# Third pair's q and k halves copied into the operands four steps later, in a one-core attention and mixture-of-experts kernel

## The chip, the cores and the metric

The kernel runs on one core of a Trainium2 chip. The metric is the time of one execution in microseconds (us) on the device. TensorE is called PE here, VectorE DVE, ScalarE ACT, GpSimd POOL and SyncE SP. SP computes nothing: it starts DMA transfers, one after the other, in the order in which the program lists them.

## What is computed

Four sequences of 768 tokens go through attention with eight heads of 64 columns. A query sees only the keys that fall to the same of 16 centroids. The result is the input of a mixture of eight experts, of which each token takes two.

```python
q_assign = np.argmax(np.einsum('bhsd,hcd->bhsc', q_n, c_n), axis=-1)
k_assign = np.argmax(np.einsum('bhsd,hcd->bhsc', k_n, c_n), axis=-1)
mask = q_assign[:, :, :, None] == k_assign[:, :, None, :]
scores = scale * np.matmul(q, k.transpose(0, 1, 3, 2))
scores = np.where(mask, scores, -1000000000.0)
scores = scores - np.max(scores, axis=-1, keepdims=True)
attn = np.exp(scores)
attn = attn / (np.sum(attn, axis=-1, keepdims=True) + 1e-09)
return np.matmul(attn, v).astype(np.float32)
# ... x = heads side by side; then, for each expert e of a token's top two:
h = np.maximum(x[mask] @ w1[e], 0.0)
out[mask] += top2_w[mask, k, None] * (h @ w2[e])
```

## The kernel before

**Pairs and steps.** Attention goes by pairs of heads, 16 in all, numbered p = 0 to 15. A pair takes 12 steps: for each of its two heads (s = 0, 1) six blocks of 128 keys. Step t computes scores and their exponentials for one block (`scores`, L506: two matmuls, one on operand A and one on operand B, for each half of the 768 queries, then an ACT exponential, L515), and adds the block of four steps earlier to the output (`values`, L529). Pair 0 owns steps 0 to 11, pair 1 steps 12 to 23, pair 2 steps 24 to 35. Everything a pair needs beforehand is laid beside the steps of the pairs ahead of it.

**What a pair needs.** `load_qk` (L316) brings q and k of four heads from HBM with two DMAs. `a_split` (L374) transposes one head's q or k on PE (L381) and splits it into a high half (ACT, L390) and a low half (DVE, L391), both written to the tile `hl`; four calls fill `hl` for a pair. `b_place` (L457) then copies `hl` within SBUF into the operands A and B of the pair, with ten DMAs on SP (all at L455, the helper `dma`). `b_mask` (L469) copies the centroid marks `mk` into A with four DMAs. `b_max` (L475) multiplies parts of A and takes row maxima on DVE (L483, L486), and `b_negT` (L497) turns the negated maxima (L500, ACT L502 into `nt`) and copies them into two rows of B with one DMA. `scores` of a head can't run on B before those two rows are in.

**Buffers.** There are three A and three B, so pair p uses number p % 3. In the order listings below, A_151, A_152 and A_153 are those of pairs 0, 1 and 2, and B_154, B_155 and B_156 likewise. `hl` exists once (pair 1 alone uses a tile called `xt`), so `a_split` of pair 3 overwrites the `hl` from which `b_place` of pair 2 copies. `qk` has two buffers. All PSUM results but the outputs go through a ring of six banks.

**What sets the order.** The table `AT` (L24) gives each call a step, relative to w = 12 * (p - 2). `attention` (L182) files the calls under their steps in thirds of a step and emits them in that order, and each engine and SP runs its own in that order. For the calls around the change the steps come out as: pair 2's `b_place` at 0.333 - 0.667 = -0.333; pair 0's second `b_negT` (maxima of its second head, first used by `scores` in step 6) at -24 + 27.333 = 3.333; `load_qk` of the second sequence's first four heads at 24 - 20.667 = 3.333; pair 2's `b_mask` at 6.333; pair 3's first `a_split` at 12 - 4.667 = 7.333; pair 2's first `b_max` at 9.333.

Of the kernel before, what the change touches and what calls it, by code (L numbers as in the profile page):

```python
# [31 lines left out]
    bmax=9.333, neg=20.333, negT=22.0, zero=27.0, zstep=12.0, zlist=15.667, store=2.667, log=1.667, log2=3.0,  # L32
    logstep=0.667, turn=7.667, list=23.0, lstep=[2.0, 2.0, 1.0], bstep=1.0,
    gate=7.667, gstep=0.333, am=5.333, amstep=0.333, ky=4.0, cut=[13, 20], gplace=17.333,
    vd=[1, 1, 2, 3, 4, 5], sec=-6.0, qf=-4.0, place1=4.333,
    fv=[{'v': -5.0, 'vscale': 13.0, 'am': 24.333, 'amstep': 0.333, 'vsplit': 25.333, 'vstep': 2.0},
        {'v': 9.0, 'vscale': 11.667, 'am': 13.333, 'amstep': 0.333, 'vsplit': 15.0, 'vstep': 1.0}],
    thr=0.333, bmax1=14.667, bstep1=0.5)
# [6 lines left out]
class Kernel:  # L45
# [136 lines left out]
    def attention(self, ctx):  # L182
# [18 lines left out]
        def at(step, f, *a):  # L201
            sched.setdefault(divmod(round(3 * step), 3), []).append((f, a))

        def chain(step, by, fs):
            for i, f in enumerate(fs):
                at(step + by * i, f)


        T = AT
        for p in range(NP):  # L210
            b, hp = divmod(p, H // 2)
            w = 12 * (p - 2)
            if hp == 0:
                for g in range(2):
                    at(w + T["qk"] + 24 * g + (T["qf"] if (b, g) == (0, 1) else 0), self.load_qk, b, g)
                    v = w + 24 * g
                    V = T["fv"][g] if p == 0 else T
                    at(v + V["v"], self.load_v, b, g)
                    for h in range(0, 4, 2):
                        at(v + V["vscale"] + V["amstep"] * h, self.v_max, b, g, h)  # L220
                    chain(v + V["am"], V["amstep"], self.v_scale(b, g))
                    for h in range(4):
                        at(v + V["vsplit"] + V["vstep"] * h, self.v_split, b, g, h)
            P = T["first"] if p == 0 else T
            w += (0, T["sec"], T["thr"])[p] if p < 3 else 0
            for i in range(4):
                at(w + P["split"][i], self.a_split, p, i // 2, i % 2)
            if p == 0:
                at(w + P["sims"][0], self.c_turn)
            at(w + P["place"] + (T["place1"] if p == 1 else 0), self.b_place, p)  # L230
            for s in range(2):
                at(w + P["sims"][s], self.a_sims, p, s)
            for s in range(2):
                at(w + P["sum"][s], self.a_sum, p, s)
            for k, f in (("max1", self.a_max1), ("ge", self.a_ge), ("ky", self.a_ky), ("max2", self.a_max2),
                         ("eq", self.a_eq), ("mask", self.a_mask), ("bmask", self.b_mask)):
                at(w + P[k], f, p)
            if p == 0:
                for s in range(2):
                    for j in range(NJ):  # L240
                        at(w + P["bmax"][s] + P["bstep"][s] * j, self.b_max, p, s, j)
                    at(w + P["neg"][s], self.b_neg, p, s, 1)
                    at(w + P["negT"][s], self.b_negT, p, s, 1)
            else:
                w = 12 * (p - 2)
                bm, bs = (T["bmax1"], T["bstep1"]) if p == 1 else (T["bmax"], T["bstep"])
                for s in range(2):
                    for j in range(NJ):
                        at(w + bm + bs * (6 * s + j), self.b_max, p, s, j)
                at(w + T["neg"], self.b_neg, p, 0, 2)  # L250
                at(w + T["negT"], self.b_negT, p, 0, 2)
            if hp == H // 2 - 1:
                z = w + 36 + L
                if b + 1 == B:
                    continue
                at(z + T["store"], self.store_x, b)
                for jj in range(NJ):
                    at(z + T["log"] + T["logstep"] * jj, self.g_logits, b, jj)
                    at(z + T["log2"] + T["logstep"] * jj, self.g_logits2, b, jj)
                at(z + T["turn"], self.g_turn, b)  # L260
                fs = self.g_gate(b)
                chain(z + T["gate"], T["gstep"], fs[:self.GP])
                chain(z + T["gplace"], T["gstep"], fs[self.GP:])
                for j in range(2 * NJ):
                    at(z + T["list"] + T["lstep"][b] * j, self.g_list, b, j)
# [26 lines left out]
        for t in range(min(sched)[0], z + L + 2):  # L292
# [8 lines left out]
            if 0 <= u < z:  # L301
                p, s, kc = u // 12, (u % 12) // 6, u % 6
# [902 lines left out]
```

## Time and profile before

| | |
|---|---|
| median of 3 runs | 1111.88 us (1110.49 to 1113.07) |
| the profiled execution | 1111.9 us, of which 1110.1 us are the span of its instructions |
| PE busy | 1044.8 us, 94% of the span |
| DVE, POOL, ACT busy | 660.2, 542.2 and 484.3 us |
| mean granted TensorE clock | 0.981 |

The span runs from the first to the last instruction of the core. The remaining 1.8 us lie around it. Busy shares are means over the whole span, while the change lies in its first tenth, so the argument reads stretches of a few microseconds there: the order of SP's DMAs, the rows of single instructions with the idle time ahead of them, and the DMA traffic and clock by the microsecond.

### The profile page before, as it was taken

The page shows a single profiled execution, that of the slowest core. Times are in us where ns is not written, and L with a number is a line of the kernel's source. Part 1 is how long each engine was busy: PE and PEld are TensorE (multiplying, and loading weights), DVE is VectorE, ACT ScalarE, POOL GpSimd, SP SyncE. Part 2 cuts the span into 40 slices and gives each one's busy share as a digit, 9 for nine tenths or more (in the row PEclk, how much of TensorE's full clock was granted, in tenths as well). Part 3 has the DMA queues.
Part 4 walks back from the last instruction along what each step waited for, and adds up shares of the span by engine and source line. Part 5 has one row for each costly group of instructions (what it writes and reads, how often), then busy time and mean ns, then how long its engine had stood idle before and what let it go on. Part 6 is the DMA issues. An engine that isn't in the chain of part 4 may idle for free.

```text
span 1110.1 us, 22397 instructions
## 1 busy us (share of the span) xinstructions
PE 1044.8 (94%) x8709; PEld 815.9 (74%) x8709; DVE 660.2 (59%) x1412; ACT 484.3 (44%) x962; POOL 542.2 (49%) x598
## 2 busy tenths in 40 slices
PE   5789999999999999889999999999999999999994
PEld 4678898889889988765775766856757668567573
DVE  5777686977697868876365435444454354444411
ACT  2457767676767676562133323232233232322300
POOL 8257675789678968712324232341242323412311
PEclk8899999999999999899999999999999999999998
DMA  7776767666757655052235324441353243422200
GB/s 205 167 176 150 174 157 198 147 175 156 202 141 183 154 143 151 13 174 100 70 120 188 105 89 144 129 152 63 124 170 100 85 148 125 153 67 87 58 32 33
DMA packets 87056, 144.46 MB, mean 130 GB/s; under 512 B 13689, under 2 KB 65273, under 8 KB 86434
## 3 DMA queue, kind: packets, MB, share of 16 engines
q1 hardware_dynamic: 73650, 106.61, 36.0%
q0 software_dynamic: 13296, 36.38, 9.9%
q8 instruction: 70, 1.15, 0.4%
q14 instruction: 40, 0.33, 0.1%
HBM read 78.21 MB, written 26.51 MB: 94 GB/s over the span
## 4 chain that ended last, share of the span: by engine, by line
PE 72%; DVE 11%; issue 8%; POOL 2%; ACT 2%; DMA 2%; SPq 1%; POOLq 0%; DVEq 0%; ACTq 0%
PE ring L1105 20%; PE ring L1144 19%; PE ring L514 9%; PE ring L483 5%; PE av L543 3%; PE av L549 2%; PE av L545 2%; PE ring L1095 2%; DVE aux L486 2%; PE ring L402 2%; PE ring L381 2%; DMA A<-mk 1%; DVE mm L486 1%; PE ring L417 1%; POOL out L1157 1%
## 5 line engine op out<-in xcount | busy, mean ns | idle before, releaser
L526 POOL TENSOR_TENSOR pl<-pe 128x768 f16<-128x768 f32 x173 | 251.8, 1470 | 82.7 <-ACT pe L515 80.5
L1105 PE MATMUL ring<-xT,w1t 128*128 128x416 f16 (+2 forms) x1536 | 274.4, 340 | 0.2 <-DVE xT L1010 0.2
L1144 PE MATMUL ring<-w2t,hT 128*128 128x512 f32 x1152 | 273.0, 393 | 0.0
L1144 PEld LDWEIGHTS ring<-w2t,hT 128*128 128x128 f32 x1152 | 213.3, 188 | 43.5
L1105 PEld LDWEIGHTS <-w1t 128*128 128x128 f16 x1536 | 149.9, 98 | 121.8 <-issue 5.4
L515 ACT ACTIVATE pe<-ring,l 128x384 f32<-128x384 f32 x384 | 201.5, 578 | 65.3 <-PE ring L514 55.7
L1157 POOL DMA_INDIRECT out<-yo,idx x52 | 62.8, 1208 | 233.6 <-DVE yo L1153 144.3
L486 DVE TENSOR_REDUCE aux<-ring 128x1 f32<-128x384 f32 x192 | 108.0, 562 | 74.5 <-PE ring L483 67.1
L514 PE MATMUL ring<-A 128*128 128x384 f32 x384 | 142.0, 370 | 0.7 <-ACT pe L515 0.7
L514 PE MATMUL ring<-B 128*128 128x384 f32 x384 | 130.6, 340 | 2.7 <-DMA B<-nt 2.7
L1153 DVE SCALAR_TENSOR_TENSOR yo<-ring,we,xt 128x512 f32<-128x512 f32 (+1 forms) x49 | 36.8, 750 | 156.5 <-PE ring L1144 133.7
L1114 ACT ACTIVATE hT<-ring 128x416 fp32r<-128x416 f32 (+3 forms) x128 | 56.7, 488 | 166.3 <-PE ring L1105 147.2
L483 PE MATMUL ring<-A 128*128 128x384 f32 x384 | 109.1, 360 | 12.1 <-DMA A<-mk 3.9
L1115 DVE SCALAR_TENSOR_TENSOR hT<-ring,hT 128x416 fp32r<-128x416 f32 (+3 forms) x128 | 66.1, 553 | 80.3 <-ACT hT L1114 74.4
L1084 POOL DMA_INDIRECT xg<-xs,idx x52 | 54.2, 1041 | 116.8 <-PE ring L1095 100.3
L486 DVE TENSOR_REDUCE mm<-ring 128x1 f32<-128x384 f32 x192 | 105.2, 548 | 0.0
L1009 ACT ACTIVATE xT<-ring,sx 128x512 f16<-128x512 f32 (+1 forms) x56 | 35.7, 653 | 150.5 <-PE ring L1095 150.5
L543 PE MATMUL av<-vv,pe 128*128 128x65 f16 x1152 | 98.0, 195 | 2.9 <-DVE xt L557 2.9
L545 PE MATMUL av<-vv,pe 128*128 128x64 f16 x1152 | 97.0, 193 | 0.0
L543 PEld LDWEIGHTS <-pe 128*128 128x128 bf16 x1152 | 80.4, 99 | 18.1 <-issue 11.8
L483 PEld LDWEIGHTS ring<-A 128*128 128x128 f32 x384 | 70.8, 193 | 24.0 <-ACT pe L515 10.1
L545 PEld LDWEIGHTS <-pe 128*128 128x128 bf16 x1152 | 78.6, 99 | 0.3
(205 smaller groups left out, 1423.8 us busy)
## 6 DMA issues: line engine op xcount, KB each, us to landing
stg<-in_moe_w SPq DMA_DIRECT2D x64, 512.0 KB
A<-hl SPq DMA_DIRECT2D x30, 384.0 KB
B<-hl SPq DMA_DIRECT2D x30, 384.0 KB
vt<-in_v SPq DMA_DIRECT2D x8, 768.0 KB
out<-zt SPq DMA_DIRECT2D x12, 512.0 KB
xs<-xt SPq DMA_DIRECT2D x4, 1536.0 KB
A<-hl SPq DMA_DIRECT2D x60, 96.0 KB
B<-hl SPq DMA_DIRECT2D x30, 192.0 KB
```

The source lines that it names most:

```text
L483: nc.tensor.matmul(t, A[:, 0, s, j * 128:j * 128 + 128], A[:, 1, s, n * 384:n * 384 + 384], start=True, stop=True)
L486: nc.vector.tensor_reduce(o, t, axis=X, op=OP.max, negate=True)
L514: nc.tensor.matmul(t, M[:, 1 - qi, s, ks], M[:, qi, s, ns], start=not qi, stop=bool(qi))
L515: nc.scalar.activation(pe[:, n], t, AF.Exp, bias=self.l64[:, 0:1], scale=self.scale)
L526: (nc.vector if last else nc.gpsimd).tensor_tensor(lo, pe, hi, op=OP.subtract)
L543: nc.tensor.matmul(av[:, j, :], ph[:, js], vv[:, hh, kj, 64:129], start=(kc == 0 and j == 0), stop=False, skip_group_check=True)
L545: nc.tensor.matmul(av[:, j, :64], ph[:, js], vv[:, hh, kj, 0:64], start=False, stop=False, skip_group_check=True)
L1105: nc.tensor.matmul(p, self.w1t[:, wi, c, f * 128:f * 128 + 128], self.xT[:, xi, c, n0:n1], start=(i == 0), stop=(i == 3 * ND - 1))
L1114: nc.scalar.activation(h0, x, AF.Relu)
L1115: nc.vector.scalar_tensor_tensor(h1, x, 0.0, h0, op0=OP.max, op1=OP.subtract)
L1144: nc.tensor.matmul(p, self.hT[:, hi, f, t * 128:t * 128 + 128], self.w2t[:, wi, f], start=(i == 0), stop=(i == 3 * NF - 1))
L1157: i = nc.gpsimd.indirect_dma_start(out=self.out, out_offset=bass.IndirectOffsetOnAxis(ap=en[:r], axis=0), in_=yo[:r], in_offset=None, boun ...
```

## The change

One number of the table goes, and a tuple takes its place. Pair 1's offset of 4.333 stays as it was; pair 0's is zero; pair 2's `b_place` moves by 4.0 steps, from -0.333 to 3.667.

```diff
-    vd=[1, 1, 2, 3, 4, 5], sec=-6.0, qf=-4.0, place1=4.333,
+    vd=[1, 1, 2, 3, 4, 5], sec=-6.0, qf=-4.0, later=(0, 4.333, 4.0),
...
-            at(w + P["place"] + (T["place1"] if p == 1 else 0), self.b_place, p)
+            at(w + P["place"] + (T["later"][p] if p < 3 else 0), self.b_place, p)
```

The lists of PE, DVE, ACT and POOL keep every instruction in its place. Only SP's list changes. Before, on SP, behind the marks of pair 1 (A_152<-mk), stood the ten copies of pair 2 (eight rows, of which the last two are shown) and then the second maxima of pair 0, the loads and the marks of pair 2:

```order
L455 DMA B_156<-hl 64x4x384
L455 DMA B_156<-hl 32x4x384
L455 DMA B_154<-nt 2x6x128
L323 DMA qk<-in_q 128x4x384
L323 DMA qk<-in_k 128x4x384
L455 DMA A_153<-mk 16x2x384 x4
```

Now, on SP, between the marks of pair 1 and the copies of pair 2 (the first four of their eight rows are shown):

```order
L455 DMA A_152<-mk 16x2x384 x4
L455 DMA B_154<-nt 2x6x128
L323 DMA qk<-in_q 128x4x384
L323 DMA qk<-in_k 128x4x384
L455 DMA A_153<-hl 64x4x384
L455 DMA A_153<-hl 32x2x384 x2
L455 DMA B_156<-hl 64x4x384
L455 DMA B_156<-hl 32x4x384
```

Three DMAs, the maxima and the two loads of 768 KB each, have moved ahead of the ten copies; the marks of pair 2 and all that follows stand behind the copies as before.

On ACT the list is the same before and now. This is the place where pair 3's first `a_split` stands, with what each instruction waits for (DMAHW are the counters of SP's DMAs, which go round eight of them):

```order
L449 ACTIVATE mk<-ring,ms 128x768 [waits DMAHW3_49,DMAHW2_49,DMAHW4_49,DMAHW1_49,PE_49]
L515 ACTIVATE pe<-ring,l_123 128x384 [waits PE_49,Pool_49]
L515 ACTIVATE pe<-ring,l_123 128x384 [waits PE_49]
L369 ACTIVATE vt<-vt,am 128x384
L370 ACTIVATE vv<-vt 128x6x64 [waits Activation_49]
L390 ACTIVATE hl<-ring 128x384 [waits DMAHW4_49,DMAHW3_49,DMAHW5_49,DMAHW2_49,DMAHW6_49,DMAHW1_49,DMAHW7_49,DMAHW0_49,PE_49]
L390 ACTIVATE hl<-ring 128x384 [waits PE_49]
```

Nothing moved here: the first L390 of pair 3 waits for all eight counters, which are those of the ten copies that read `hl`, and the copies are what has moved on SP.

## Rows read from the trace of the kernel before

**Rows 1.** Cores' view, and the page's line of PE busy times.

```profile
core 0: 1110.1 us, clock 0.981
PE 1044.8 (94%) x8709; PEld 815.9 (74%) x8709; DVE 660.2 (59%) x1412; ACT 484.3 (44%) x962; POOL 542.2 (49%) x598
```

**Rows 2.** Chain that ended last, 55 to 100 us: start, us, what.

```profile
58.28 3.67 DMA B<-nt
...
62.00 1.33 PE ring L514 x3
...
68.42 0.48 ACT hl L390
68.93 0.57 DVE hl L391
...
69.54 0.71 PE ring L483 x2
```

**Rows 3.** SP's timeline: start, us, engine, line, operation, out<-in, count.

```profile
23.48 0.58 SPq L323 DMA_DIRECT2D qk<-in_q  x1
24.10 0.56 SPq L323 DMA_DIRECT2D qk<-in_k  x1
...
47.64 2.91 SPq L455 DMA_DIRECT2D A<-hl  x3
...
56.89 1.29 SPq L455 DMA_DIRECT2D B<-hl  x2
58.28 1.30 SPq L455 DMA_DIRECT2D B<-nt  x1
...
65.72 3.06 SPq L455 DMA_DIRECT2D A<-mk  x4
69.52 0.37 SPq L331 DMA_DIRECT2D vt<-in_v  x1
74.27 0.67 SPq L455 DMA_DIRECT2D B<-nt  x1
...
76.76 2.86 SPq L455 DMA_DIRECT2D A<-hl  x3
```

**Rows 4.** ACT's timeline, at pair 0's second maxima.

```profile
52.82 0.25 ACT L502 ACTIVATE nt<-ring 12x128 fp32r<-12x128 f32 x1
```

**Rows 5.** PE's timeline; in brackets the idle time before and its releaser.

```profile
35.98 0.82 PE L447 MATMUL ring<-identb,oh 128*128 128x128 bf16 x6 [3.04 <-DVE oh L438]
...
49.09 0.66 PE L483 MATMUL ring<-A 128*128 128x384 f32 x2 [1.75 <-POOL pl L526]
...
62.00 0.69 PE L514 MATMUL ring<-B 128*128 128x384 f32 x1 [2.74 <-DMA B<-nt]
...
69.01 0.33 PE L514 MATMUL ring<-B 128*128 128x384 f32 x1
...
72.72 0.51 PE L483 MATMUL ring<-A 128*128 128x384 f32 x2
```

**Rows 6.** By microsecond: us, PE, PEld, DVE, ACT, POOL busy, PEclk, DMA share, GB/s.

```profile
41.00:42.00 1.00, 1.00 (x6) 1.00 (x6) 1.00 (x3) 0.23 (x1) 0.00 (x0) 0.80 0.96 241
...
60.00:61.00 1.00, 0.00 (x0) 0.00 (x0) 0.00 (x0) 0.00 (x0) 0.49 (x1) 1.00 0.88 186
...
62.00:63.00 1.00, 1.00 (x3) 1.00 (x4) 0.00 (x0) 0.22 (x1) 0.00 (x0) 0.50 0.90 333
63.00:64.00 1.00, 1.00 (x7) 0.69 (x6) 0.32 (x1) 0.94 (x2) 0.00 (x0) 0.50 1.12 402
64.00:65.00 1.00, 1.00 (x17) 1.00 (x16) 0.70 (x2) 0.33 (x1) 0.92 (x1) 0.50 1.03 384
65.00:66.00 1.00, 1.00 (x16) 1.00 (x14) 0.18 (x1) 0.66 (x1) 0.55 (x1) 0.85 1.02 359
66.00:67.00 1.00, 1.00 (x8) 0.96 (x7) 0.97 (x3) 0.59 (x2) 0.00 (x0) 1.00 0.11 30
...
90.00:91.00 1.00, 1.00 (x31) 1.00 (x28) 1.00 (x3) 0.62 (x2) 1.00 (x1) 1.00 0.27 62
```

## The prediction, made before the changed kernel ran

> **What bounds the kernel now.** I read the busy times first: PE is busy for 94% of the span at a mean clock of 0.981 [rows 1], so for most of the run a delay of PE at one place is a delay of the end. The change moves only SP's DMAs around 48 to 70 us, so I then followed the chain that ended last through that stretch. It goes through SP: the ten copies of pair 2 hold SP from 47.64 to 58.18 us, the DMA of pair 0's second maxima is started behind them at 58.28 and lands 3.67 us later, and PE goes on at 62.00 [rows 2, 3]. ACT had those maxima ready at 52.82 + 0.25 = 53.07 us [rows 4]. PE's row at 62.00 names the price: 2.74 us idle, waiting for B<-nt [rows 5]. There is a second price in the clock column: the granted clock is 0.50 of full, which is the 1.2 GHz level, in the three microseconds after that idle time, 0.85 in the fourth and 1.00 from 66 us [rows 6]. That is 3.3 us at half speed behind the restart, with PE busy throughout, so some 1.65 us of work were lost. So the wait costs 2.74 + 1.65 = 4.4 us in all.
>
> Then I looked for who waits for the ten copies. The order listing says it: pair 3's first split, L390 on ACT, waits for all of them, since it overwrites the `hl` they read. In the trace before it starts at 68.42, and the first low half (L391 on DVE) follows; PE's next matmul behind them starts at 69.54 [rows 2]. The copies were long done by then: the maxima queued right behind them had landed at 58.28 + 3.67 = 61.95. So this wait costs nothing now, with 6.5 us to spare.
>
> **What the change removes.** The maxima no longer stand behind the copies. SP is free from the marks of pair 1 on, so their DMA starts at about 53.1 us. PE wants them at 62.00 - 2.74 = 59.26, 6 us later; even the 3.67 us of the queued case fits. The idle time goes and so does the drop of the clock: 4.4 us by the time PE and ACT come to pair 3's first split. ACT would be there at 68.42 - 4.4 = 64.0 us.
>
> **What it adds.** The copies now start later and behind more. SP starts the maxima at 53.1 (0.7 us, as the row at 74.27), then the two loads of q and k (0.58 and 0.56 us as at 23.48 and 24.10), then the first copy at about 55.2 us [rows 3]. How long do ten copies take? Before, 47.64 to 61.95 = 14.3 us [rows 2, 3]. Pair 3's went from 76.76 to about 90.3, by the microsecond in which the traffic ends, that is 13.5 us [rows 3, 6]. They are bound by the traffic, not by SP: at 186 GB/s the DMA engines were already 0.88 busy [rows 6]. If nothing else were in the way they would end at 55.2 + 14.3 = 69.5 us. But the two loads are now ahead of them. Before, these ran behind the copies, in 62.0 to 66.1, 4.1 us at a DMA share of 0.9 to 1.1 [rows 6], so they leave no room beside them. They are started 1.3 us ahead of the first copy, so they push the copies back by 4.1 - 1.3 = 2.8 us: the end is at 72.3 us.
>
> The lowest end I see is 55.2 + 13.5 = 68.7 (the shorter row and no delay by the loads), the highest 55.2 + 14.3 + 4.1 = 73.6 (no head start). I take 72.3, because the maxima of before, the one DMA that stood behind other traffic in this stretch, landed only when that traffic was over.
>
> **The new wait.** ACT comes to L390 at 64.0 and can start it at 72.3. Its queue is in order, so the exponentials of the following steps stand behind it; DVE waits in L391 likewise, with maxima queued behind; PE's ring of six banks fills with what these two don't take away. PE can finish step 8's scores (the last at 69.01 + 0.33 before, so about 65.0 now [rows 5]) and then stands still until L390 and L391 are through, 69.54 - 68.42 = 1.1 us after L390 starts. That is some 8.4 us of idle PE, in place of the 2.74 that went.
>
> Compared at the same instruction, L390 is at 72.3 instead of 68.42: **+3.9 us**, bounds 68.7 - 68.42 = +0.3 and 73.6 - 68.42 = +5.2. This comparison already contains the 4.4 us gained, since the end of the copies, not ACT's arrival, decides.
>
> **The clock.** After 2.74 and 3.04 us of idle PE the clock was at 0.50, after 1.75 us it was not [rows 5, 6]. So 8.4 us will halve it again, now behind the restart. In the row at 41 us (0.80) the half-speed stretch that began before PE's restart at 35.98 ends at about 41.4, so there it lasted 5.4 us, 2.7 us of work. I take **+1.65 us**, the loss of the case at 62 us, since it is the same work and nearest; bounds 0 and +2.7.
>
> **Other queues moved past.** Pair 2's marks still stand behind the copies on SP. Before they started at 65.72 [rows 3], waiting for ACT. Now they follow the copies and their data (196 KB of small rows) comes behind them, at about 72.3 + 1 = 73.4 us. The first matmul that reads them (pair 2's first maxima, at 72.72 before [rows 5]) comes 3.2 us behind the one at 69.54, that is at 72.72 + 3.9 + 1.65 = 78.3 now: covered by 5 us. If that cover were gone it would cost what it is late, microsecond for microsecond. The v load (69.52 before) starts at about the same time as before and is needed later. The loads of q and k arrive earlier, which nobody waits for. POOL stands still with the others and its work is no more than before.
>
> **Sum.** Profiled execution 1111.9 us (span 1110.1), next to the median of 1111.88: +3.9 + 1.65 = +5.5, so **1117.4 us**. By the bounds of the two terms +0.3 to +7.9, 1112.2 to 1119.8. What follows is driven by the same chain (SP's next DMA of maxima waits for ACT, the copies of pair 3 wait for that), and PE is nearly full from there, so I expect nothing to give the delay back.
>
> **Rivals.**
> *Faster: the copies are quick.* If ten copies within SBUF moved as fast as the loads do (333 to 402 GB/s in 62 to 66 us [rows 6], twice the 186 of the copies), 13.4 us of traffic would be 6.5, and with the loads not in the way they would be done at 55.2 + 1 + 6.5 = 62.7, ahead of ACT's 64.0. Then the whole 4.4 us is kept: 1107.5 us. It decides in favour of this if the copies end within 8.8 us of their first start. Against it stand both rows, 13.5 and 14.3, and a DMA share of 0.88 at 186 GB/s.
> The Trainium skill, page "DMA: Bandwidth & Descriptors", section "Where 436 GB/s comes from", says that transfers from SBUF to SBUF are bound by the fabric at 435 GB/s; by that an estimate of 3.9 MB for the loads and copies would be over in some 9 us, which gives about 1108 us. The trace doesn't agree: in the copies it moved 186 GB/s at a DMA share of 0.88.
>
> *Same: a break-even.* The copies run beside the loads and end at 68.7 to 69.5, and the clock's drop costs no more than a microsecond. Then L390 is 0.3 to 1.1 us later than before and the result is 1112.2 to 1114. For it: the bound of 68.7 exists. Against it: DMA shares add up to over 1, and PE would still stand for over 4 us, more than the 2.74 that halved the clock.
>
> *Slower than forecast: the marks are last.* If the marks landed after 78.3 us, pair 2's maxima would wait too. They are started at about 70 us behind the tail of the copies; landing 3 us beyond the point would give 1120.4. The 3.67 us that the maxima took behind the copies [rows 2] speaks against it.
>
> **How the numbers follow.** Forecast 0.75; faster rival 0.06; same 0.12; marks last or a long half-speed stretch 0.07. The difference that a measurement of this kernel can tell is about 0.2%, 2.2 us: faster means under 1109.7, slower over 1114.1. From the cases: faster 0.06, same 0.12, slower 0.82. The range leaves out the faster rival, half of the same case and most of the slowest: 1113.0 to 1120.0.
>
> **What would show it.** Right: PE's idle time ahead of B<-nt near 59 us is gone and the clock stays at 1.00 there; SP's ten copies start near 55 and pair 3's L390 near 72 us after a long idle time of ACT, with PE, DVE and POOL idle too; then a clock of 0.50 for some microseconds. Wrong: L390 before 68 us (the copies were quicker, or the loads don't delay them); or the delay at L390 is there and the end isn't late, which would mean slack further on that I haven't seen.

## The result and the profile after

The changed kernel takes 1120.34 us (median of 6 runs, 1118.49 to 1122.21) against 1112.05 us of the kernel before in the same set: a ratio of 1.0079, 95% interval 1.0063 to 1.0095. It is slower, as forecast, by 8.3 us where 5.5 were forecast, and just outside the range that ended at 1120.0. A second set gave 1119.77 us, ratio 1.0064 (1.0048 to 1.0081). The profiled execution took 1120.32 us.

The cores' view of after, beside the first line of [rows 1]:

```profile
core 0: 1118.5 us, clock 0.975
```

SP's timeline of after (start, us, engine, line, operation, out<-in, count), beside [rows 3]:

```profile
52.81 0.67 SPq L455 DMA_DIRECT2D B<-nt  x1
53.58 0.38 SPq L323 DMA_DIRECT2D qk<-in_q  x1
54.02 0.49 SPq L323 DMA_DIRECT2D qk<-in_k  x1
54.56 2.08 SPq L455 DMA_DIRECT2D A<-hl  x3
...
64.27 1.69 SPq L455 DMA_DIRECT2D B<-hl  x2
66.07 3.85 SPq L455 DMA_DIRECT2D A<-mk  x4
70.01 0.53 SPq L331 DMA_DIRECT2D vt<-in_v  x1
81.51 0.68 SPq L455 DMA_DIRECT2D B<-nt  x1
```

The maxima of pair 0 start 5.5 us earlier than before and the copies 6.9 us later. PE's timeline of after, beside [rows 5], and the chain that ended last, beside [rows 2]:

```profile
58.81 0.33 PE L514 MATMUL ring<-B 128*128 128x384 f32 x1
...
75.01 1.01 PE L483 MATMUL ring<-A 128*128 128x384 f32 x2 [9.57 <-DVE hl L391]
...
79.96 0.51 PE L483 MATMUL ring<-A 128*128 128x384 f32 x2
```

```profile
65.35 8.38 DMA B<-hl
73.88 0.50 ACT hl L390
74.40 0.57 DVE hl L391
75.01 1.01 PE ring L483 x2
```

The row at 58.81 is the matmul on B that waited 2.74 us before: it has no idle time ahead of it now. The row at 75.01 is the one that stood at 69.54 before. It has 9.57 us of idle time, and the chain goes through the last of the ten copies, which lands at 65.35 + 8.38 = 73.73 us, and through pair 3's first split right behind it. ACT's own row of that split, the first high half of pair 3, shows the wait from ACT's side:

```profile
73.88 0.87 ACT L390 ACTIVATE hl<-ring 128x384 fp32r<-128x384 f32 x2 [9.50 <-DMA A<-mk]
```

ACT came to it at 73.88 - 9.50 = 64.38 us. This row names the marks of pair 2 (A<-mk) as the releaser, the chain names the copies. The marks follow the copies on SP and use the same eight counters, and the profile infers its releasers; in the first experiment L390 starts before all of the marks are started, so it doesn't need them. By the microsecond (columns as in [rows 6]):

```profile
53.00:54.00 1.00, 1.00 (x6) 0.71 (x5) 0.90 (x3) 0.87 (x2) 1.00 (x2) 1.00 0.00 0
54.00:55.00 1.00, 0.85 (x4) 0.35 (x3) 1.00 (x3) 0.29 (x2) 1.00 (x2) 1.00 0.55 48
55.00:56.00 1.00, 0.48 (x3) 0.47 (x3) 1.00 (x3) 0.47 (x1) 1.00 (x2) 1.00 0.73 218
56.00:57.00 1.00, 0.51 (x3) 0.19 (x1) 1.00 (x3) 0.82 (x2) 0.46 (x1) 1.00 1.07 404
...
58.00:59.00 1.00, 1.00 (x18) 1.00 (x15) 0.89 (x3) 0.00 (x0) 1.00 (x2) 1.00 0.88 278
...
67.00:68.00 1.00, 0.00 (x0) 0.00 (x0) 0.00 (x0) 0.00 (x0) 0.00 (x0) 1.00 1.08 231
...
70.00:71.00 1.00, 0.00 (x0) 0.00 (x0) 0.00 (x0) 0.00 (x0) 0.00 (x0) 0.50 1.14 191
...
76.00:77.00 1.00, 1.00 (x14) 0.94 (x13) 1.00 (x3) 0.30 (x1) 1.00 (x1) 0.50 0.00 0
78.00:79.00 1.00, 1.00 (x5) 1.00 (x4) 0.47 (x2) 0.49 (x1) 0.00 (x0) 0.50 0.00 0
79.00:80.00 1.00, 1.00 (x7) 1.00 (x7) 0.46 (x1) 0.54 (x2) 0.00 (x0) 0.96 0.00 0
```

All five engines' columns are at zero around 67 to 71 us while the DMA engines are full; the granted clock halves during the wait (0.50, the 1.2 GHz level) and stays there until about 79 us, 4 us behind PE's restart.

### The profile page after: what moved, and what is told of

Read it like the earlier page. It is cut to its first block, busy times and chain, and to the rows that moved or that the text cites. A ratio compares the mean times of both kernels' runs of the same rounds, so it can differ in the third digit from the quotient of the medians.

```text
span 1118.5 us, 22393 instructions
## 1 busy us (share of the span) xinstructions
PE 1048.3 (94%) x8709; PEld 817.7 (73%) x8709; DVE 660.6 (59%) x1412; ACT 484.8 (43%) x962; POOL 542.7 (49%) x598
## 4 chain that ended last, share of the span: by engine, by line
PE 73%; DVE 11%; issue 8%; DMA 2%; POOL 2%; ACT 2%; SPq 1%; POOLq 0%; DVEq 0%; ACTq 0%
PE ring L1105 20%; PE ring L1144 19%; PE ring L514 9%; PE ring L483 5%; PE av L543 3%; PE av L549 2%; PE av L545 2%; PE ring L381 2%; PE ring L402 2%; PE ring L1095 2%; DVE aux L486 2%; PE ring L417 1%; DVE mm L486 1%; SPq L455 1%; POOL out L1157 1%
```

## The experiments

The theory: pair 3's first split waits for the end of pair 2's copies, and the two loads that now stand ahead of the copies push that end out. The rivals: copies that are started late are slow by themselves; something behind them in the queue delays their landing; the clock, not the wait, makes the loss. All experiments are read by one number, the time from SP's first copy of pair 2 to the start of the split's first L390 on ACT (19.3 us in the changed kernel, 54.56 to 73.88), because that number does not depend on when an execution reaches this place.

**Loads behind the copies.** The copies move by 3.667 instead of 4.0 steps, which puts them ahead of the loads.

```diff
-    later=(0, 4.333, 4.0),
+    later=(0, 4.333, 3.667),
```

> Pair 2's copies stand behind pair 0's second maxima as in the change, but ahead of the two loads of q and k instead of behind them. Theory (pair 3's first split waits for the end of the copies, and the loads ahead of them pushed that end out): the copies start at 53.6 us and end 14.3 us later, so the split's L390 starts near 67.9 instead of 73.88 us; PE still idles about 4 us, the clock still halves, and the time is about 1 us over the kernel before, near 1113 us. Rival A (the loads don't matter, copies started this late are slow by themselves, 19 us as in the changed kernel): L390 near 72.8 and about 1119 us. Rival B (the dependence of the split on the copies is not what costs): the time stays at 1120 us.

Rows of this kernel's SP and ACT timelines:

```profile
55.12 2.95 SPq L455 DMA_DIRECT2D A<-hl  x3
...
68.41 2.51 SPq L455 DMA_DIRECT2D A<-mk  x4
```

```profile
69.53 0.87 ACT L390 ACTIVATE hl<-ring 128x384 fp32r<-128x384 f32 x2 [3.56 <-DMA B<-hl]
```

That is 14.4 us, against 19.3: the loads ahead of the copies cost the difference. L390 starts at 69.53 while SP is still starting the marks (68.41 to 70.92), so it is not the marks that it waits for. The time was another matter: 1117.15 us, ratio 1.0049 (1.0035 to 1.0063), not 1113. The marks of pair 2 now stand behind the loads; pair 1's maxima were started at 78.56 us, 1.9 us later than in the timed profile of the next kernel, and the halved clock lasted from 70 to 77 us. The timed runs also scatter from 1114 to 1119 us, and of that the one profile (1114.98 us) shows only the lower end, so why the median is 4 us over the forecast is not fully explained.

**Loads far behind.** The loads go to the other side of pair 1's maxima, so that only marks and the v load follow the copies.

```diff
-  at(w + T["qk"] + ..., self.load_qk, b, g)
+  at(10.333 if (b, g) == (1, 0) else w + T["qk"] + ..., self.load_qk, b, g)
```

> As the change, but the two loads of q and k go far behind, to the other side of pair 1's maxima, so that nothing but marks and the v load follows the copies. Theory: copies from 53.6 us, L390 near 67.9 us, as with the loads right behind. Rival (transfers queued behind the copies also push their end out): L390 earlier here than with the loads right behind, by up to 2 us. If the tail is pushed out by the marks and the v load alone, L390 is near 69.5 in both.

> The kernel with the two loads behind pair 1's maxima again, now timed, as the reference of the next. L390 14.5 us behind the first copy, about 1113.8 us.

Rows of the second, timed kernel's profile:

```profile
55.02 2.97 SPq L455 DMA_DIRECT2D A<-hl  x3
```

```profile
69.44 0.87 ACT L390 ACTIVATE hl<-ring 128x384 fp32r<-128x384 f32 x2 [3.48 <-DMA A<-mk]
```

First copy to L390 took 55.38 to 69.92 = 14.5 us in one profile and 55.02 to 69.44 = 14.4 us in the other, timed at 1112.88 us, ratio 1.0013 (1.0001 to 1.0024). So loads that follow the copies don't delay them (the marks and the v load follow them in both kernels), and moving the copies alone, without the loads ahead, costs about 1 us: the wait at the split (PE idle 3.52 us) is then a little longer than the 2.74 us that the change removed.

**The v load later.** To see whether the v load behind the marks delays the last copy, it goes behind pair 1's maxima.

```diff
-  {'v': 9.0, 'vscale': 11.667, ...
+  {'v': 10.333, 'vscale': 11.667, ...
```

> As the change, with one more move: the v load that followed pair 2's marks goes behind pair 1's maxima, so that it is not in the queue while the copies end. In the changed kernel the last copy landed at 73.73 us although the traffic up to 72 us already covers loads, copies and marks. If the v load delayed that landing, L390 starts near 72.2 us here; if not, at 73.9 us as before. The v load itself now comes late for the maxima of v, which can cost some 2 us further on and says nothing on the question.

56.15 to 74.76 = 18.6 us. The unchanged order gave 19.3 and, in its second profile below, 18.5. The v load is not the cause. The total of 1123.99 us, a single run, contains the later maxima of v (PE idle 2.2 us for them).

**Loads earlier.** The loads go ahead of pair 0's maxima, where SP was idle, so they are through before the copies start.

```diff
+  at(2.667 if (b, g) == (1, 0) else w + T["qk"] + ..., self.load_qk, b, g)
```

> As the change, but the two loads of q and k go ahead of pair 0's second maxima on SP, so they are started some 5 us earlier and are through before the copies start. Theory (the loads cost only while they are in the queue ahead of the copies): first copy to pair 3's L390 takes 14.4 us, as with the loads behind (14.4 and 14.5 us measured), against 19.3 in the change; the marks of pair 2 have no loads ahead of them either, so about 1113.5 us. Rival (what costs is that the copies come late on SP, whatever is ahead of them): 19 us from the first copy to L390 and 1120 us.

```profile
54.01 2.96 SPq L455 DMA_DIRECT2D A<-hl  x3
```

```profile
69.38 0.87 ACT L390 ACTIVATE hl<-ring 128x384 fp32r<-128x384 f32 x2 [3.35 <-DMA A<-mk]
```

That is 15.4 us, and the time is 1114.59 us, ratio 1.0033 (1.0015 to 1.0051). Late copies are not slow by themselves: that rival falls. The loads were started 6.2 us ahead of the first copy here, and their traffic ended as it was started: nearly all of their cost is gone. The 0.9 us over 14.5 are not explained.

**Half the load.** Only the load of q stays ahead of the copies. The load of k, left out of `load_qk` here, becomes a call of its own, `load_k` (not shown), behind pair 1's maxima.

```diff
+                    if (b, g) == (1, 0):
+                        at(10.333, self.load_k, b, g)
...
+                if i and (b, g) == (1, 0):
+                    continue
```

> As the change, but only the load of q stays ahead of the copies; the load of k goes behind pair 1's maxima. Theory (the copies end later by the whole traffic of what was queued ahead, with no allowance for the head start): first copy to L390 takes 14.4 + 2.1 to 2.4 = 16.5 to 16.8 us. If a head start counted, as I reckoned in the prediction, half the load would be through by then and it would be about 15.3.

```profile
54.51 3.15 SPq L465 DMA_DIRECT2D A<-hl  x3
```

```profile
71.42 0.87 ACT L400 ACTIVATE hl<-ring 128x384 fp32r<-128x384 f32 x2 [6.54 <-DMA A<-mk]
```

16.9 us; the total of this single run is 1119.28 us. With nothing ahead the time is 14.46 (mean of three profiles), with one load 16.9, with both 19.04 (mean of the five profiles with the loads ahead as in the change, 18.5 to 19.9): 2.4 and 4.6 us more, for 2.05 and 4.1 us of load traffic. The copies end later by all of the traffic ahead of them and a little more; the half microsecond more is not explained. The Trainium skill, page "DMA: Bandwidth & Descriptors", section "Queues, rings and completion order", says that each DMA engine consumes descriptors in ring order. These numbers agree with it.

**The changed kernel again.**

> The changed kernel once more, for a second profile of it beside the others of this set. In the first, 1.6 of the 8.4 us by which its span is longer arise near 563 us, where a 2.0 us wait that both kernels have was followed by a halved clock in one and not in the other. If that is chance, a second profile may be without it: 6.8 us over the profiled kernel before; if the change causes it, it is there again. L390 of pair 3 again 19.3 us behind the first copy.

55.66 to 74.17 = 18.5 us; PE idle 8.2 us ahead of the restart. The clock fell again behind the 2.0 us wait near 565 us. That doesn't settle whether the change causes it, and the place is taken up below.

**PE kept busy.** 46, and then 52, matmuls that nobody reads stand on PE ahead of pair 3's first transposes.

```diff
+        at(7.333, self.keep_busy)
...
+    def keep_busy(self):
+        A = self.A[0]
+        for i in range(52):
+            self.nc.tensor.matmul(self.aux[:, 0:384], A[:, 1, 0, 0:128], A[:, 0, 0, 0:384], start=True, stop=True)
```

> As the change, with 46 extra matmuls of 384 columns on PE ahead of pair 3's first transposes, some 8 us of work that nobody reads, laid into the time in which PE would wait for the copies. The wait for the copies stays as it is (L390 19 us behind the first copy). Theory (the halved clock after the wait costs 1.65 to 1.8 us on its own): the granted clock stays at 1.00 behind L390, and the time is 1.7 us under that of the changed kernel, near 1118.5 us or a ratio of 1.006 to the kernel before. Rival (the clock costs nothing there, another engine sets the pace): as the changed kernel, 1.008. If the extra matmuls overrun the wait, pair 3's first split is late by that much and the time is longer.

> The changed kernel with 52 instead of 46 extra matmuls on PE in the wait. With 46, PE still idled 1.69 us ahead of the restart and the clock fell 1.3 us behind it, for 3.2 us. With 52 the idle time is under 1 us. Theory (the halved clock behind the wait costs 1.65 to 1.8 us): the clock stays at 1.00 behind the restart and the time is 1.7 us or more under that of the changed kernel in this set. Rival: the clock falls all the same or costs nothing, no difference.

With 46 the aim was missed in the profile: PE still idled 1.69 us and the clock was at 0.50 from 78 to 81 us. That execution, 1120.93 us, is the slowest of eight; their median is 1117.65 us, ratio 1.0050 (1.0036 to 1.0064), and what the clock did in the faster ones is not known. With 52, PE's row at the restart and the clock behind it:

```profile
75.09 0.70 PE L489 MATMUL ring<-A 128*128 128x384 f32 x2 [0.35 <-DVE hl L397]
```

```profile
76.00:77.00 1.00, 1.00 (x24) 1.00 (x22) 1.00 (x3) 0.49 (x1) 1.00 (x1) 1.00 0.11 26
78.00:79.00 1.00, 1.00 (x12) 0.71 (x11) 1.00 (x3) 1.00 (x3) 0.00 (x0) 1.00 0.00 0
```

The wait for the copies is the same (55.02 to 73.95 = 18.9 us), the clock stays at 1.00, and the time is 1116.97 us, 2.8 us under the changed kernel's 1119.77 in the same set. No run of the one reaches a run of the other (1116.01 to 1118.28 and 1119.42 to 1122.21). 52 matmuls of useless work make the kernel faster: the halved clock behind the wait is a loss of its own. SP's start of pair 1's maxima, which waits for PE's and ACT's work behind the restart, shows how much of it lies in this stretch:

```profile
79.97 0.68 SPq L461 DMA_DIRECT2D B<-nt  x1
```

From L390 to this start it is 79.97 - 73.95 = 6.0 us, against 5.85 in the kernel before and 7.6 and 8.4 in the two profiles of the changed kernel: 1.6 to 2.4 us. The rest of the 2.8 is not accounted for; part of it can be the place near 565 us, where the clock did not fall in this profile. The ratio with 52 is still 1.0040 (1.0025 to 1.0054), 5.2 us over the kernel before, so the rival that the clock, not the wait, makes the loss falls.

**Pair 3's own halves.** As the kernel with the loads far behind, but pair 3's halves are written into the idle qk buffer, not over the `hl` from which the copies read.

```diff
   self.st[p]["hl"] = (self.gp.tile([128, 4, 2, 384], F32R, name="xt", bufs=1) if p == 1 else
+                      self.pre.tile([128, 4, 2, 384], F32R, name="qk", bufs=2) if p == 3 else
```

> As the kernel with the loads far behind, with one more edit: pair 3's halves are written into the idle buffer of qk instead of the hl from which pair 2's copies read, so that pair 3's first split no longer waits for the copies. Theory: L390 starts near 64 us instead of 69.9 and the clock stays at 1.00 there; then pair 2's first maxima, which need the copies and the marks behind them, become the wait: wanted near 68.3, there near 71, so 2.7 us of the gain are given back. About 1110 us, 3 to 4 us under the reference. Rival (the overwritten hl is not what the split waits for): no difference.

```profile
64.12 1.00 ACT L391 ACTIVATE qk<-ring 128x384 fp32r<-128x384 f32 x2
```

```profile
69.02 0.76 PE L484 MATMUL ring<-A 128*128 128x384 f32 x2 [0.26 <-issue]
```

The split starts at 64.12, with no wait, where the prediction had put ACT's arrival (64.0), and PE goes on at a clock of 1.00. So the overwritten `hl` is what the split waits for. PE's longest idle time there, at 69.02, is 0.26 us: the wait that I expected of pair 2's maxima for copies and marks is all but absent. Pair 1's maxima are started at 70.82, against 76.67 in its reference, 1.66 us of which lie ahead of this stretch: near 49 us PE had waited 2.33 us for pair 1's marks in the reference, with the clock at 0.50 from 50 to 53 us behind it, and 1.45 us here, with the clock at 1.00. But the timed gain is small: 1111.91 us, ratio 0.9998 (0.9980 to 1.0016), with runs from 1108.2 to 1117.1. The profile shows one of the fast ones (1108.75). The mechanism is shown; the 3 to 4 us are not.

**Copies in halves.** Two versions of the kernel before, in which five copies stay where they were and five follow pair 0's maxima; in the second the loads also go behind pair 2's marks.

```diff
-  at(w + P["place"] + (T["place1"] if p == 1 else 0), self.b_place, p)
+  for a in range(2):
+      at(3.333 if (p, a) == (2, 1) else w + P["place"] + (T["place1"] if p == 1 else 0), self.b_place, p, a)
...
-        for a in range(2):
+        for a in (half,):
```

> The kernel before, with pair 2's ten copies cut in two: five where they were, then pair 0's second maxima, then the other five, then the loads. Theory: the maxima start at about 53.1 and land by 57, so the 2.74 us of idle PE near 59 us and the halved clock behind it go; the copies end at about 62.5 us, ahead of the 64.0 us at which pair 3's first split comes, so no new wait: 4.4 us off the kernel before, about 1107.7 us. Rival (marks of pair 2 behind the loads come too late for pair 2's first maxima near 68.3 us): 2 us of that are given back there, 1109.5. If the copies still end after 64 us, it is microsecond for microsecond less.

> The kernel before, with pair 2's copies cut in two around pair 0's second maxima, and with the two loads of q and k behind pair 2's marks instead of ahead of them. With the halves alone, PE no longer waited for the maxima, but waited 1.47 us for the marks, which were started at 63.3 us behind the loads and landed 7.7 us later. Theory: the marks now land by 67 us, that wait goes, and the time is about 1.5 us under the halves' 1109.9, near 1108.4. Rival (the v load behind the loads comes late for the maxima of v, or a DMA further on takes the place): no better than the halves alone.

The first takes 1109.88 us, ratio 0.9978 (0.9967 to 0.9990), and is faster than both kernels. PE has neither wait, but one further on, as its rival foresaw. PE's rows there, first of the halves, then of the halves with the loads later:

```profile
71.56 0.59 PE L484 MATMUL ring<-A 128*128 128x384 f32 x2 [1.47 <-DMA A<-mk]
```

```profile
74.04 0.44 PE L515 MATMUL ring<-B 128*128 128x384 f32 x1 [0.67 <-DMA B<-nt]
```

With the loads behind the marks the wait for the marks goes, and pair 1's maxima, now behind loads and v load, take its place with 0.67 us. The profiled execution took 1108.51 us, but the median of 12 runs is 1110.49, ratio 0.9992 (0.9974 to 1.0011): no better than the halves alone.

## Why the prediction was right or wrong, point by point

**What bounds the kernel, and the wait that goes: right.** The idle time of 2.74 us ahead of the matmul on B is gone and the clock is at 1.00 behind it. ACT's arrival, forecast at 64.0 us, was 64.38 in the changed kernel, and L390's start was 64.12 in the kernel with pair 3's own halves.

**The new wait: right in mechanism and place.** The order's waits named it: ACT in L390, DVE in L391, PE still between step 8's scores and the next maxima, 9.57 us where 8.4 were forecast.

**The end of the copies: the term that was mis-sized.** I forecast 55.2 + 14.3 + 2.8 = 72.3 us; it was 73.73. The first copy started at 54.56, 0.6 us earlier than reckoned. The 14.3 us of the copies alone were right (14.4 and 14.5 measured). The 2.8 us for the loads were wrong: I subtracted a head start of 1.3 us from their 4.1 us of traffic, as if the loads were moving at full rate while SP was still starting DMAs. They were not: the rows from 53 to 57 us show no traffic in 53 to 54, though the loads are started at 53.58 and 54.02, 48 GB/s in the microsecond of the first copy's start (54.56), 218 in the next, and 404, the rate of the loads before (402, [rows 6]), only from 56 on. Measured, the loads cost 4.6 us. The case that I had set as the upper bound (55.2 + 14.3 + 4.1 = 73.6) is the one that happened; the earlier start and the half microsecond that the loads cost beyond 4.1 cancel. L390 came 73.88 - 68.42 = 5.46 us later instead of 3.9, which is 1.6 of the 2.9 us by which the profiled spans differ more than forecast (8.4 and 5.5).

**The clock: right, in size partly by luck.** 1.65 us were forecast. SP's start of pair 1's maxima moved from 74.27 [rows 3] to 81.51, by 7.24 us, of which 7.24 - 5.46 = 1.78 arose behind the restart. The kernel with busy PE, where this part takes 0.17 us more than before instead of 1.78, shows that it is the clock. The second profile of the changed kernel gave 2.56 by the same sum, and the v load later 2.02, so the closeness to 1.65 is chance.

**"I expect nothing to give the delay back": not quite.** In pair 4's part 0.9 us come back. Before, PE waited there 1.43 us for marks; after, it stood for 0.51, for which the row names no releaser. PE's rows, before and after:

```profile
126.84 0.59 PE L483 MATMUL ring<-A 128*128 128x384 f32 x2 [1.43 <-DMA A<-mk]
```

```profile
133.33 0.59 PE L483 MATMUL ring<-A 128*128 128x384 f32 x2 [0.51 <-issue]
```

From there the difference is 6.5 us, and 6.8 up to 530 us. So the copies and the clock make 6.8 us of the 8.4 by which the spans differ.

**What the sum did not have.** The other 1.6 us arise at one place near 563 us, in the experts. Rows of PE and of the clock, before (556.86) and after (563.68):

```profile
556.86 0.27 PE L1020 MATMUL ring<-ident,wm 128*4 128x128 f32 x1 [1.97 <-DVE wm L1042]
```

```profile
563.68 0.33 PE L1020 MATMUL ring<-ident,wm 128*4 128x128 f32 x1 [1.97 <-DVE wm L1042]
```

```profile
556.00:560.00 4.00, 3.14 (x23) 2.21 (x24) 2.18 (x7) 0.83 (x3) 0.62 (x1) 1.00 0.47 131
```

```profile
563.00:567.00 4.00, 3.31 (x13) 1.77 (x13) 1.51 (x5) 0.22 (x1) 0.45 (x1) 0.60 0.41 126
```

The idle time is the same to a hundredth, but behind it the clock stayed at 1.00 before and fell to 0.60 on the mean of four microseconds after. All 14 profiles have this wait with 1.97 or 1.98 us. The clock fell behind it in four: in both of the changed kernel, in the half load and in the timed profile of the loads far behind. It did not in the v load later and in both kernels with busy PE, which reach this place as late as the changed kernel. So being late doesn't cause it by itself, and whether the change makes it likelier stays open. It fits the runs, without being shown by them: 1111.9 + 6.8 = 1118.7 is where the lowest two of the six runs lie (1118.49 and 1118.64); the others are 1.7 us and more above. So two things together carried the profiled execution past 1120.0: the mis-sized end of the copies, and this fall, which stood in no term and whose cause is open. With either of them alone it would have stayed within the range.

**The rivals.** The faster one needed copies that end within 8.8 us of their first start; without loads they take 14.4. The figure of 435 GB/s for transfers within SBUF, which the Trainium skill gives on its page "DMA: Bandwidth & Descriptors", section "Where 436 GB/s comes from", and which I had set beside this rival, is not reached: in the row at 67 us, late in the copies, the DMA engines moved 231 GB/s at a share of 1.08. The break-even is nearly what the kernel with the loads far behind does (1.0013): it needed the loads out of the way, not beside the copies. The marks were not last in the changed kernel (PE's first maxima of pair 2, at 79.96 us, have no idle time ahead of them); they were in the halves (1.47 us). That this rival's 1120.4 is nearly the measured 1120.34 is chance.

## What to carry to other kernels

Moving a transfer later to free another must be costed at both ends: who waits for what it writes, and who waits to overwrite what it reads. Count everything that is queued ahead of it at the traffic it still has to move: here loads started 1 us ahead of the copies cost all of theirs, and loads started 6.2 us ahead 0.9 us. When a wait long enough to halve the clock can't be avoided, look at what PE could do in it.

## What the runs showed of the hardware that was not expected

The prediction had a row with 1.75 us of idle PE behind which the clock stayed at 1.00. That does not make idle times of about that length safe. With 46 extra matmuls, 1.69 us of idle PE were followed by a clock of 0.50. The same 1.97 us near 563 us were followed by a fall in four profiles of 14. At the very place of the row with 1.75 us, near 49 us, PE idled 1.23 to 2.33 us; behind it the clock fell in eight of the 14 profiles and stayed in six, and 1.94 us stand in both groups. A fall cost 1.6 us near 563 us, and 1.8 to 2.6 behind pair 3's split. That is near the 0.2%, 2.2 us, that a measurement of this kernel can tell, and it can happen at each of these places or not; a part of the scatter of the runs is likely to be that, which the timed runs, without profiles, don't show.

Loads from HBM and copies within SBUF on one queue gained nothing here from being in flight together: loads with 4.1 us of traffic, started just ahead of the copies, put the copies' end off by 4.6 us.
